# LSH attention, MLP and experts on one core: the sums' transposes and the marks' projections placed behind the products with v, two casts per pair of heads placed behind exponentials

## Chip, cores and metric

The kernel runs on one core of a Trainium2 chip. What counts is the device time of one execution in microseconds; the runs of a kernel are compared by their median. The engines are TensorE (PE; its weight loads are listed apart as PEld), VectorE (DVE), ScalarE (ACT), GpSimd (POOL), and SyncE (SP), which issues most transfers.

## What is computed

Three stages: attention with a mask from hashed buckets, a SiLU MLP, and a layer of eight experts of which each chosen token uses one. The change lies in the first stage, of which this is the reference:

```python
B, H, S, D = q.shape                      # 2, 8, 768, 64
scale = 1.0 / np.sqrt(D)
q_bits = (np.einsum('bhsd,dk->bhsk', q, proj) > 0).astype(np.int64)   # 6 bits
k_bits = (np.einsum('bhsd,dk->bhsk', k, proj) > 0).astype(np.int64)
q_bucket = np.sum(q_bits * powers, axis=-1)
k_bucket = np.sum(k_bits * powers, axis=-1)
mask = q_bucket[:, :, :, None] == k_bucket[:, :, None, :]
scores = np.where(mask, scale * np.matmul(q, k.transpose(0, 1, 3, 2)), -1000000000.0)
scores = scores - np.max(scores, axis=-1, keepdims=True)
attn = np.exp(scores)
attn = attn / (np.sum(attn, axis=-1, keepdims=True) + 1e-09)
return np.matmul(attn, v).astype(np.float32)
```

Behind it come `g = silu(x @ w_in)`, `g @ w_out`, and for the tokens with `x @ w_skip > 0` the expert with the largest gate. All results are float32.

## The kernel before

The sixteen heads are eight pairs i of two heads. Each pair has two halves of its queries; such a half is a unit u (16 in all), and a unit is six steps s: three query tiles of 128 for each of two heads. So there are 96 steps (NS), twelve to a pair; m is the step's place in its pair, and j = s % 3.

A step computes the scores of 128 queries with 768 keys (`em_S`, L407: four matmuls into one of two S buffers in PSUM), their maximum (`em_max`, L412, DVE), the exponential with its sum (`em_exp`, L420, ACT), later the transpose of the probabilities (`em_T`, L431) in groups of three 128x128 pieces, three pieces to one tile "T" in PSUM, and the copy of each T tile into PT in SBUF (`em_C`, L441), some on ACT, some on DVE. In the steps with j = 0 and j = 2 PE turns three T tiles; in those with j = 1 it multiplies a half of a unit's PT with v instead (`em_PV`, L449: 12 instructions, into 64 columns of the array for each head).

Everything runs in the order in which the code is written, engine by engine; nothing is rescheduled. S(s) needs the exponential of step s - 2, since there are two S buffers. The T tiles come from a ring of three PSUM buffers (`tag="T", bufs=3`), which the two kinds of tile below share:

- **rT**: the six reciprocals of a unit's sums (`em_rc`, L453 and L454, in place) are transposed on PE (`em_r`, L460), copied by ACT to r (L462), written to DRAM and read back as rb, spread over the rows; `em_x` multiplies with it on POOL. It stands at the end of step s = 11 + 6u, a step with j = 2.
- **pj**: the bits of the next pair. `prep_proj` (L355) makes four projections, each into 32 columns of the array, and `marked` (L359, DVE) turns them into marks mb, from which seven small DMAs fill rows of Q2 and K2 (`prep_rows`, at m = 4). It stands at the end of the step m = 2, also j = 2.

The next pair's operands are made meanwhile: `PRE` lists the steps m in which ACT casts a head's k and q to K1 and Q1 (L334 and L336, "kh" and "qa"), `POST` those in which DMAs copy them on ("k2", "qb") and POOL subtracts for the low parts ("kl", "ql"). In a step these casts stand ahead of the exponential:

```python
            for mm, *op in PRE[i == 0]:
                if nxt and mm == m:
                    prep_op(i + 1, *op)
            if j == 0 and s <= NS:
                em_C(n0 + 1, onA)
            if s < NS:
                mx = em_max(s)
            if j == 0 and s <= NS:
                em_C(n0, onD)
            if s < NS:
                em_exp(s, mx)
```

In the last third of the attention `hook` slips in the conversion of the first MLP weights (L219 on ACT, L220 to L228 on DVE). `busy` is a zeroed tile that keeps PE at work during the first loads.

Of the kernel before, what the change touches and what calls it, by code (L numbers as in the profile page):

```python
# [9 lines left out]
F32 = mybir.dt.float32  # L10
F32R = mybir.dt.float32r
BF16 = mybir.dt.bfloat16
# [7 lines left out]
P = 128  # L20
# [6 lines left out]
def kernel(  # L27
# [16 lines left out]
    nc = tc.nc  # L44
# [6 lines left out]
    HQ = S // 2  # L51
    QT = HQ // P
# [33 lines left out]
    ident = cp.tile([P, P], F32, name="ident")  # L86
# [190 lines left out]
    def attention(hook):  # L277

        mainp, main_st = opened("a_main")
        evp, ev_st = opened("a_even")  # L280
        topp, top_st = opened("a_top")
        psTV, psTV_st = opened("a_psTV", space=PSUM, side="right")
        psS, psS_st = opened("a_psS", space=PSUM)

        raws, ops, vts, mks = {}, {}, {}, {}
# [64 lines left out]
        def prep_proj(i):  # L350

            ps = psTV.tile([P, HQ], F32, tag="T", name="pj", bufs=3)
            for j in range(4):
                t = raws[i][1 - j // 2]
                nc.tensor.matmul(ps[32 * j:32 * j + 32], prj[j // 2], t[:, (j % 2) * HQ:(j % 2 + 1) * HQ], start=True, stop=True)  # L355
            marked(mks[i], ps, slice(0, P))

        def marked(dst, ps, r):
            nc.vector.tensor_scalar(dst, ps[r], c_m[r, 0:1], c_m[r, 1:2], op0=ALU.is_gt, op1=ALU.mult)  # L359
# [28 lines left out]
        units = [(i, qh) for i in range(B * NP) for qh in range(2)]  # L388
# [4 lines left out]
        NS = len(steps)  # L393
        st_P, st_T, st_sum, st_pv, st_none = {}, {}, {}, {}, {}
# [20 lines left out]
        def em_exp(s, mx):  # L415
            u, qt, hd = steps[s]
            if qt == 0 and hd == 0:
                st_sum[u] = mainp.tile([P, 2 * QT], F32, name="sums", bufs=4)
            pt = mainp.tile([P, S], F32, name="P", bufs=3)
            nc.scalar.activation(pt.rearrange("p (a b) -> p a b", a=2), Ss[s % 2][:, :, 0:HQ], AF.Exp, bias=mx,  # L420
                                 accum_out=st_sum[u][:, hd * QT + qt:hd * QT + qt + 1])
            st_P[s] = pt
# [13 lines left out]
        def em_C(n, copy):  # L436
            if not 0 <= n < 2 * NS:
                return
            s, half = divmod(n, 2)
            u, qt, hd = steps[s]  # L440
            copy(PTs[u % 2][:, hd, half * (KT // 2):(half + 1) * (KT // 2), qt * P:(qt + 1) * P], st_T.pop(n))  # L441

        def em_PV(u, ks):
            i, qh = units[u]
            if 0 in ks:
                st_pv[u] = psTV.tile([P, HQ + 1], F32, tag="V", name="pv", bufs=1)
            for k in ks:
                for hd in range(2):
                    nc.tensor.matmul(st_pv[u][hd * D:(hd + 1) * D], vts[i][:, k, hd], PTs[u % 2][:, hd, k],  # L449
                                     start=(k == 0), stop=(k == KT - 1))  # L450

        def em_rc(u):
            nc.vector.tensor_scalar(st_sum[u], st_sum[u], 1e-9, None, op0=ALU.add)  # L453
            nc.vector.reciprocal(st_sum[u], st_sum[u])  # L454

        def em_r(u):

            sums = st_sum.pop(u)
            ps = psTV.tile([P, HQ], F32, tag="T", name="rT", bufs=3)
            nc.tensor.transpose(ps[0:2 * QT, 0:P], sums, ident)  # L460
            r = mainp.tile([2 * QT, P], F32, name="r", bufs=2)
            nc.scalar.copy(r, ps[0:2 * QT, 0:P])  # L462
            nc.sync.dma_start(r_d[u], r)
            rb = mainp.tile([P, HQ], F32, name="rb", bufs=2)
            for hd in range(2):
                nc.sync.dma_start(rb[hd * D:(hd + 1) * D], r_d[u:u + 1, hd * QT:(hd + 1) * QT].rearrange("o t p -> o (t p)").to_broadcast([D, HQ]))
            return rb

        def em_out(u):

            x = mainp.tile([P, HQ], F32, name="x", bufs=2)
            nc.scalar.activation(x, st_pv.pop(u)[:, 0:HQ], AF.Identity, bias=st_none.pop(u))
            return x
# [16 lines left out]
                eng.tensor_tensor(lo[:, c], x[:, c], hi[:, c].bitcast(F32), op=ALU.subtract)  # L490


        busy = mainp.tile([P, P], BF16, name="busy", bufs=1)
        nc.vector.memset(busy, 0.0)
        bs = psTV.tile([P, P], F32, tag="V", name="bs", bufs=1)

        def em_busy(n):
# [38 lines left out]
        prep_load(1)  # L536
        nc.sync.dma_start(ct[:, 66:NC + P], consts[:, 66:NC + P])
        prep_op(0, 1, "scale", nc.scalar)
        prep_proj(0)
        prep_op(0, 1, "kh", nc.scalar)  # L540
        nc.scalar.copy(Q1[r, 0, c1], qs[r, c1])
        nc.gpsimd.tensor_copy(Q1[o, 0, c1], qs[r, c1])
# [14 lines left out]
        for t in PTs:  # L557
            nc.gpsimd.memset(t[:, :, :, HQ:HQ + 1], 1e-9 / S)

        PRE = [[(c[j], j // 2, w, nc.scalar) for j, w in enumerate(("kh", "qa", "kh", "qa"))]  # L560
               for c in ((0, 3, 6, 9), (3, 5, 7, 9))]

        POST = [[(c[j], j // 4, w, None if w in ("k2", "qb") else nc.gpsimd)
                 for j, w in enumerate(("k2", "kl", "qb", "ql") * 2)]
                for c in ((0, 1, 3, 4, 6, 6, 9, 9), (3, 4, 5, 6, 7, 8, 9, 10))]
        rbs, xs = {}, {}
        onA, onD = nc.scalar.copy, nc.vector.tensor_copy
        for s in range(NS + PU + 4):
            i, m = divmod(s, 2 * PU)
            nxt = i + 1 < B * NP  # L570
            p, j = divmod(s, 3)
            n0 = 6 * p - 5 + (0, 3, 3)[j]
            if nxt and m == 0:
                prep_alloc(i + 1)
            if s < NS:
                if s > 1:
                    em_S(s)
            if j == 0 and s <= NS:
                for n in range(3):
                    em_T(n0 + n)  # L580
            u, g = divmod(s - 10, 6)
            if j == 1 and s < NS and u >= 0:
                em_PV(u, (0, 1, 2) if g == 0 else (3, 4, 5))
            if s == NS:
                em_PV(len(units) - 2, (3, 4, 5))
            if s == NS + 3:
                em_PV(len(units) - 1, range(KT))
            if j == 2 and s < NS or s == NS + 1:
                for n in range(3):
                    em_T(n0 + n)  # L590
                em_C(n0, onA)
                em_C(n0 + 1, onA)
            u, g = divmod(s - 15, 6)
            if g == 0 and 0 <= u < len(units) - 2:
                xs[u] = em_out(u)
            if s == NS + 4:
                xs[len(units) - 1] = em_out(len(units) - 1)
            for mm, *op in PRE[i == 0]:
                if nxt and mm == m:
                    prep_op(i + 1, *op)  # L600
            if j == 0 and s <= NS:
                em_C(n0 + 1, onA)
# [3 lines that stand above are left out]
                em_C(n0, onD)  # L606
            if s < NS:
                em_exp(s, mx)
            if j == 1 and s < NS:
                em_C(n0 - 1, onD)  # L610
            if s == NS:
                em_C(n0 + 2, onD)
            if j == 2 and s < NS:
                em_C(n0 + 2, onD)
            if s == 1:
                prep_op(1, 0, "scale", nc.scalar)
            u, g = divmod(s - 8, 6)
            if g == 0 and 0 <= u < len(units):
                em_rc(u)
            u, g = divmod(s - 14, 6)  # L620
            if g == 0 and 0 <= u < len(units) - 2:
                em_none(u)
            if s == NS + 3:
                em_none(len(units) - 1)
            u, g = divmod(s - 11, 6)
            if s < NS and g == 0 and u >= 0:
                rbs[u] = em_r(u)
            u, g = divmod(s - 17, 6)
            if g == 0 and 0 <= u < len(units) - 1:
                em_x(u, xs.pop(u), rbs.pop(u), nc.gpsimd)  # L630
            if nxt:
                if m == (2 if i else 5):
                    prep_proj(i + 1)
                for mm, *op in POST[i == 0]:
                    if mm == m:
                        prep_op(i + 1, *op)
                if m == (4 if i else 8):
                    prep_rows(i + 1)
                if m == 0 and i + 2 < B * NP:
                    prep_load(i + 2)  # L640
                if m == (9 if i else 11) and i + 2 < B * NP:
                    prep_op(i + 2, 0, "scale", nc.gpsimd)
                if m == 11 and i + 2 < B * NP:
                    load_v(i + 2)
                if m == 11 and i + 2 == B * NP:
                    top_st.close()
            if s == NS - 2 * PU:
                ev_st.close()
            if s == NS:
                em_none(len(units) - 2)  # L650
                xs[len(units) - 2] = em_out(len(units) - 2)
            hook(s - NS)
            if s == NS + PU - 1:
                rbs[len(units) - 1] = em_r(len(units) - 1)
            if s == NS - 1:
                psS_st.close()
        em_x(len(units) - 1, xs.pop(len(units) - 1), rbs.pop(len(units) - 1), nc.gpsimd)
# [277 lines left out]
    with tc.manual_schedule():  # L935
# [130 lines left out]
        ps = ps_tile("pr", [P, 512], "O3")  # L1066
# [352 lines left out]
```

## Time and profile before

| | before |
|---|---|
| median of 3 runs | 607.8 us (607.42 to 609.62) |
| profiled execution | 607.77 us, its span 606.0 us |
| PE busy | 595.2 us (98%) |
| PEld busy | 466.3 us (77%) |
| DVE, ACT, POOL busy | 458.4, 392.1, 188.2 us |
| granted TensorE clock, mean | 0.997 of full speed |

The span is what the trace covers of the profiled execution. PE's busy time counts each matmul with a modelled end, and those overlap; how closely PE's work follows on itself is read from the starts, in the time line. A row of the time line names start, duration, engine, line, operation and tiles, how many were merged (x9), and in brackets the engine's idle time before it and what ended that.

### The profile page before, as it was taken

Reading aid. Unit: us, or ns where it says so; the run is one execution under the profiler, and the core shown is the slowest. Engines: PE = TensorE matmul, PEld = TensorE weight load, DVE = VectorE, ACT = ScalarE, POOL = GpSimd, SP = SyncE. Lnnn points to the kernel's source line nnn. Section 1 sums busy time; section 2 is a strip of 40 time slices with the busy share of each in tenths; the row PEclk is TensorE's granted clock in tenths of the full one; section 3 lists DMA queues with packets and bytes.
Section 4 is the critical chain, followed back from the end, with each engine's and each line's share of the span. In section 5 each row is a group of like instructions: output and inputs, shape, how many; then the busy total and the mean of one; then the engine's idle time right before and its main releaser. Section 6 shows DMA issues by size and latency. Waiting matters only on the chain. (4 is left out here: it accounts for less than half of the span.)

```text
span 606.0 us, 9594 instructions
## 1 busy us (share of the span) xinstructions
PE 595.2 (98%) x3311; PEld 466.3 (77%) x3311; DVE 458.4 (76%) x830; ACT 392.1 (65%) x664; POOL 188.2 (31%) x269
## 2 busy tenths in 40 slices
PE   8999999999999999999999999999999999999996
PEld 6677677676777767888888888888888887888885
DVE  6767767776777777998847985548876649999993
ACT  6878777877877775666544336344445565788872
POOL 7655664657564233300000000300000406344401
PEclk9999999999999999999999999999999999999998
DMA  6541725335131315566423000014231247999960
GB/s 168 147 133 45 202 73 154 104 110 138 48 82 43 129 53 180 189 180 210 158 99 138 1 0 2 1 60 150 104 106 69 53 140 259 321 405 407 405 259 28
DMA packets 31366, 84.13 MB, mean 139 GB/s; under 512 B 6294, under 2 KB 9942, under 8 KB 31186
## 3 DMA queue, kind: packets, MB, share of 16 engines
q1 hardware_dynamic: 29138, 79.44, 39.8%
q0 software_dynamic: 1952, 3.92, 1.9%
q8 instruction: 27, 0.44, 0.3%
q14 instruction: 25, 0.20, 0.1%
q10 hardware_dynamic: 224, 0.13, 0.1%
HBM read 67.92 MB, written 8.50 MB: 126 GB/s over the span
## 5 line engine op out<-in xcount | busy, mean ns | idle before, releaser
L412 DVE TENSOR_REDUCE mx<-S 128x1 f32<-128x770 f32 x96 | 91.8, 957 | 54.6 <-PE S L407 49.3
L260 DVE TENSOR_TENSOR wlo<-wraw,whi 128x1024 fp32r<-128x1024 f32 x100 | 119.7, 1224 | 5.5 <-ACT whi L257 5.0
L257 ACT CAST whi<-wraw 128x1024 fp32r<-128x1024 f32 x100 | 101.6, 1053 | 11.4 <-DVE wraw L228 10.2
L690 ACT ACTIVATE g<-ph 128x512 f32<-128x512 f32 x48 | 28.7, 598 | 106.9 <-PE ph L684 103.0
L420 ACT ACTIVATE P<-S,mx 128x768 f32<-128x768 f32 x96 | 86.8, 905 | 12.3 <-DVE mx L412 11.3
L407 PE MATMUL S<-K,Q 88*128 88x384 f32 (+1 forms) x384 | 91.6, 360 | 2.5 <-ACT P L420 2.0
L407 PEld LDWEIGHTS S<-K,Q 88*128 88x128 f32 (+1 forms) x384 | 62.4, 189 | 27.0 <-issue 18.8
L431 PE MATMUL T<-ident,P 128*128 128x128 f32 x576 | 74.4, 273 | 0.4 <-ACT r L462 0.2
L692 DVE TENSOR_TENSOR gl<-g,gh 128x512 fp32r<-128x512 f32 x48 | 33.2, 691 | 51.9 <-ACT gh L691 51.9
L431 PEld LDWEIGHTS T<-ident,P 128*128 128x128 f32 x576 | 66.8, 141 | 4.1 <-ACT r L462 0.8
L449 PE MATMUL pv<-PT,v 128*64 128x385 f32 x384 | 69.0, 495 | 0.0
L441 ACT COPY PT<-T 128x384 f32<-128x384 f32 x96 | 42.8, 482 | 32.7 <-PE T L431 32.0
L839 POOL DMA_INDIRECT id_d<-tk,slot x12 | 15.7, 1312 | 141.3 <-DVE pre L849 137.9
L348 POOL TENSOR_TENSOR Q<-raw,Q 64x192 fp32r<-64x192 f32 x64 | 36.5, 597 | 54.2 <-ACT Q L336 50.2
L441 DVE COPY PT<-T 128x384 f32<-128x384 f32 x96 | 52.9, 552 | 0.4 <-PE T L431 0.3
L684 PE MATMUL ph<-xhi,whi 128*128 128x512 f32 x192 | 52.2, 393 | 0.0
L684 PE MATMUL ph<-xlo,whi 128*128 128x512 f32 x192 | 51.4, 389 | 0.0
L684 PE MATMUL ph<-xhi,wlo 128*128 128x512 f32 x192 | 51.3, 389 | 0.0
L449 PEld LDWEIGHTS pv<-PT,v 128*64 128x64 f32 x384 | 24.9, 136 | 31.1 <-issue 30.1
L740 DVE CUSTOM_DVE_ANT_0 junk<-x,gwb 128x512 bf16<-128x512 f32 x72 | 45.3, 687 | 0.0
L684 PEld LDWEIGHTS ph<-xlo,whi 128*128 128x128 f32 x192 | 36.0, 188 | 7.6
L684 PEld LDWEIGHTS ph<-xhi,wlo 128*128 128x128 f32 x192 | 36.0, 188 | 7.5
(208 smaller groups left out, 1053.5 us busy)
## 6 DMA issues: line engine op xcount, KB each, us to landing
wraw<-in_w_dram SPq DMA_DIRECT2D x64, 512.0 KB
w<-in_mw_dram SPq DMA_DIRECT2D x32, 512.0 KB
v<-in_vt_dram SPq DMA_DIRECT2D x8, 384.0 KB
rb<-r_d SPq DMA_DIRECT2D x32, 96.0 KB
x_d<-x SPq DMA_DIRECT2D x12, 256.0 KB
out_dram<-x SPq DMA_DIRECT2D x12, 256.0 KB
K<-K SPq DMA_DIRECT2D x15, 192.0 KB
Q<-Q SPq DMA_DIRECT2D x15, 192.0 KB
```

The costliest lines, as they stand in the source:

```text
L257: nc.scalar.copy(hi[:, sl], t[:, sl])
L260: eng.tensor_tensor(lo[:, sl], t[:, sl], hi[:, sl].bitcast(F32), op=ALU.subtract)
L348: eng.tensor_tensor(Q2[0:D, hd, c], raws[i][1][r, c], Q1[r, hd, c].bitcast(F32), op=ALU.subtract)
L407: nc.tensor.matmul(ps[:, c, 0:HQ], q_[0:n, hd, q0:q0 + P], k_[0:n, hd, c * HQ:(c + 1) * HQ], start=first, stop=not first)
L412: nc.vector.tensor_reduce(mx, Ss[s % 2][:, :, 0:HQ + 1], axis=AX.XY, op=ALU.max, negate=True)
L420: nc.scalar.activation(pt.rearrange("p (a b) -> p a b", a=2), Ss[s % 2][:, :, 0:HQ], AF.Exp, bias=mx, accum_out=st_sum[u][:, hd * QT + qt: ...
L431: nc.tensor.transpose(ps[:, j], st_P[s][:, k * P:(k + 1) * P], ident)
L441: copy(PTs[u % 2][:, hd, half * (KT // 2):(half + 1) * (KT // 2), qt * P:(qt + 1) * P], st_T.pop(n))
L449: nc.tensor.matmul(st_pv[u][hd * D:(hd + 1) * D], vts[i][:, k, hd], PTs[u % 2][:, hd, k], start=(k == 0), stop=(k == KT - 1))
L684: nc.tensor.matmul(p_[:, 0:c1 - c0], w[:, k * P:(k + 1) * P], x[:, k, t0 * P + c0:t0 * P + c1], start=(q == 0), stop=(q == len(ops3) - 1))
L692: nc.vector.tensor_tensor(gl[:, c0:c1], g[:, c0:c1], gh[:, c0:c1].bitcast(F32), op=ALU.subtract)
L740: nc.vector.tensor_tensor_reduce(junk, xts[t], pools["gwb_t"][:, c], op0=ALU.mult, op1=ALU.add, scale=1.0, scalar=0.0, accum_out=L[:, t, c ...
```

## The change

The reciprocals go into a tile `rec` of 128 columns, zero beyond the six, and the whole tile is transposed right behind the first group of products with v of a unit (s = 10 + 6u, j = 1); ACT's copy to r and its DMAs follow the exponential of that same step. The projections of pairs 2 and up are placed right behind the second group of products (m = 1), and their marks behind that step's exponential and copy; pair 1's stay where they were. Of the casts of pairs 2 and up, those of m = 3 and 9 are placed in m = 4 and 7, and there behind the exponential; their followers in `POST` move along. `busy` becomes a view of `rec`.

```diff
@@ prep_proj
-            marked(mks[i], ps, slice(0, P))
+            return ps
...
         def em_rc(u):
             nc.vector.tensor_scalar(st_sum[u], st_sum[u], 1e-9, None, op0=ALU.add)
-            nc.vector.reciprocal(st_sum[u], st_sum[u])
-
-        def em_r(u):
-
-            sums = st_sum.pop(u)
+            nc.vector.reciprocal(rec[:, 0:2 * QT], st_sum.pop(u))
+
+        def em_rT():
             ps = psTV.tile([P, HQ], F32, tag="T", name="rT", bufs=3)
-            nc.tensor.transpose(ps[0:2 * QT, 0:P], sums, ident)
+            nc.tensor.transpose(ps[:, 0:P], rec, ident)
+            return ps
+
+        def em_r(u, ps):
+
             r = mainp.tile([2 * QT, P], F32, name="r", bufs=2)
             nc.scalar.copy(r, ps[0:2 * QT, 0:P])
             nc.sync.dma_start(r_d[u], r)
...
-        busy = mainp.tile([P, P], BF16, name="busy", bufs=1)
-        nc.vector.memset(busy, 0.0)
+        rec = mainp.tile([P, P], F32, name="rec", bufs=1)
+        nc.vector.memset(rec, 0.0)
+        busy = rec.bitcast(BF16)[:, 0:P]
...
         PRE = [[(c[j], j // 2, w, nc.scalar) for j, w in enumerate(("kh", "qa", "kh", "qa"))]
-               for c in ((0, 3, 6, 9), (3, 5, 7, 9))]
+               for c in ((0, 4, 6, 7), (3, 5, 7, 9))]
...
-                for c in ((0, 1, 3, 4, 6, 6, 9, 9), (3, 4, 5, 6, 7, 8, 9, 10))]
+                for c in ((0, 1, 4, 4, 6, 6, 7, 8), (3, 4, 5, 6, 7, 8, 9, 10))]
...
             if j == 1 and s < NS and u >= 0:
                 em_PV(u, (0, 1, 2) if g == 0 else (3, 4, 5))
+                if g == 0:
+                    rT = em_rT()
+                if nxt and m == 1 and i:
+                    pj = prep_proj(i + 1)
...
-            for mm, *op in PRE[i == 0]:
-                if nxt and mm == m:
+            casts = [op for mm, *op in PRE[i == 0] if nxt and mm == m]
+            if j != 1 or i == 0:
+                for op in casts:
                     prep_op(i + 1, *op)
...
             if s < NS:
                 em_exp(s, mx)
+            u, g = divmod(s - 10, 6)
+            if s < NS and g == 0 and u >= 0:
+                rbs[u] = em_r(u, rT)
+            if j == 1 and i:
+                for op in casts:
+                    prep_op(i + 1, *op)
             if j == 1 and s < NS:
                 em_C(n0 - 1, onD)
+            if nxt and m == 1 and i:
+                marked(mks[i + 1], pj, slice(0, P))
...
-            u, g = divmod(s - 11, 6)
-            if s < NS and g == 0 and u >= 0:
-                rbs[u] = em_r(u)
...
-                if m == (2 if i else 5):
-                    prep_proj(i + 1)
+                if m == 5 and not i:
+                    marked(mks[1], prep_proj(1), slice(0, P))
...
             if s == NS + PU - 1:
-                rbs[len(units) - 1] = em_r(len(units) - 1)
+                rbs[len(units) - 1] = em_r(len(units) - 1, em_rT())
```

On PE, the first unit with both moves, before (steps 10 to 14; S_109 and S_110 are the two S buffers, "x9" is three T tiles):

```order
L449 MATMUL pv<-PT_111,v 64x385 x6
L407 MATMUL S_110<-K_132,Q_131 128x384 x2
L407 MATMUL S_110<-K_107,Q_133 128x384 x2
L431 MATMUL T<-ident,P 128x128 x9
L460 MATMUL rT<-ident,sums 6x128
L407 MATMUL S_109<-K_252,Q_251 128x384 x2
...
L449 MATMUL pv<-PT_111,v 64x385 x6
L407 MATMUL S_109<-K_252,Q_251 128x384 x2
L407 MATMUL S_109<-K_108,Q_253 128x384 x2
L431 MATMUL T<-ident,P 128x128 x9
L355 MATMUL pj<-raw,ct 32x384 x4
```

The same stretch of PE after the change:

```order
L449 MATMUL pv<-PT_111,v 64x385 x6
L458 MATMUL rT<-ident,rec 128x128
L407 MATMUL S_110<-K_132,Q_131 128x384 x2
L407 MATMUL S_110<-K_107,Q_133 128x384 x2
L431 MATMUL T<-ident,P 128x128 x9
...
L449 MATMUL pv<-PT_111,v 64x385 x6
L355 MATMUL pj<-raw,ct 32x384 x4
L407 MATMUL S_109<-K_252,Q_251 128x384 x2
L407 MATMUL S_109<-K_108,Q_253 128x384 x2
L431 MATMUL T<-ident,P 128x128 x9
```

Both extra tiles move from behind nine transposes to behind six products, ahead of the next S; rT grows from 6 rows of output to 128.

On ACT, the steps m = 3 to 7 of the second pair, before (K_502 and Q_501 are K1 and Q1 of the next pair):

```order
L472 ACTIVATE x<-pv,none 128x384
L336 CAST Q_501<-raw 64x768
L441 COPY PT_111<-T 128x3x128
L420 ACTIVATE P,sums<-S_110,mx 128x768
L420 ACTIVATE P,sums<-S_109,mx 128x768
L441 COPY PT_111<-T 128x3x128 x2
L420 ACTIVATE P,sums<-S_110,mx 128x768
L462 COPY r<-rT 6x128
L334 CAST K_502<-raw 64x768
```

The same steps of ACT after the change, up to the second cast that moves:

```order
L474 ACTIVATE x<-pv,none 128x384
L441 COPY PT_111<-T 128x3x128
L420 ACTIVATE P,sums<-S_110,mx 128x768
L420 ACTIVATE P,sums<-S_109,mx 128x768
L464 COPY r<-rT 6x128
L336 CAST Q_501<-raw 64x768
L441 COPY PT_111<-T 128x3x128 x2
L420 ACTIVATE P,sums<-S_110,mx 128x768
L334 CAST K_502<-raw 64x768
L441 COPY PT_111<-T 128x3x128
...
L420 ACTIVATE P,sums<-S_110,mx 128x768
L336 CAST Q_501<-raw 64x768
```

The casts to Q1 stand no longer between x and a copy that an exponential waits behind, but between an exponential and the copies of the next step's T tiles, the first of them behind the copy to r.

## Rows read from the trace of the kernel before

**Rows 1.** Busy time by stage: us, then each engine's busy time, 24 to 223 us.

```profile
24.00:223.00 199.00, 198.12 (x1304) 141.07 (x1304) 144.20 (x248) 154.18 (x329) 110.69 (x179) 1.00 0.36 99
```

**Rows 2.** Time line of PEld, a T group and the next S.

```profile
105.40 1.08 PEld L431 LDWEIGHTS T<-ident,P 128*128 128x128 f32 x9
106.45 0.65 PEld L407 LDWEIGHTS S<-K,Q 128*128 128x128 f32 x4
```

**Rows 3.** Waits of PEld for other engines, 215 to 592 us: total, times, longest.

```profile
PEld L803 <- DVE oh L791: 0.7, 1, 0.7
...
PEld ey L1209 <- DVE wlo L260: 0.3, 1, 0.3
```

**Rows 4.** Time line of PEld around rT, two units.

```profile
97.16 1.08 PEld L431 LDWEIGHTS T<-ident,P 128*128 128x128 f32 x9
...
98.40 0.19 PEld L407 LDWEIGHTS S<-K,Q 128*128 128x128 f32 x1
...
137.63 1.08 PEld L431 LDWEIGHTS T<-ident,P 128*128 128x128 f32 x9
...
138.94 0.65 PEld L407 LDWEIGHTS S<-K,Q 128*128 128x128 f32 x4
```

**Rows 5.** Waits of PEld, 24 to 215 us: total, times, longest.

```profile
PEld S L407 <- ACT P L420: 4.4, 6, 0.8
PEld rT L460 <- ACT PT L441: 1.6, 10, 0.2
PEld pj L355 <- ACT PT L441: 1.0, 6, 0.2
```

**Rows 6.** Time line of PEld around pj.

```profile
89.84 1.08 PEld L431 LDWEIGHTS T<-ident,P 128*128 128x128 f32 x9
91.08 0.16 PEld L355 LDWEIGHTS pj<-raw,ct 128*32 128x32 f32 x8 [0.17 <-ACT PT L441]
91.87 0.64 PEld L407 LDWEIGHTS S<-K,Q 128*128 128x128 f32 x4 [0.62 <-issue]
```

**Rows 7.** Time line of PEld, the end of a pv group and S.

```profile
95.47 0.14 PEld L449 LDWEIGHTS pv<-PT,v 128*64 128x64 f32 x2 [0.18 <-issue]
95.79 0.14 PEld L449 LDWEIGHTS pv<-PT,v 128*64 128x64 f32 x2 [0.18 <-issue]
96.53 0.64 PEld L407 LDWEIGHTS S<-K,Q 128*128 128x128 f32 x4 [0.60 <-issue]
```

**Rows 8.** Time line of PEld, two waits for ACT.

```profile
109.63 0.65 PEld L407 LDWEIGHTS S<-K,Q 128*128 128x128 f32 x4 [0.79 <-ACT P L420]
...
113.25 0.31 PEld L431 LDWEIGHTS T<-ident,P 128*128 128x128 f32 x3 [0.30 <-ACT r L462]
```

**Rows 9.** Time line of PEld at the attention's end.

```profile
217.46 1.08 PEld L431 LDWEIGHTS T<-ident,P 128*128 128x128 f32 x9
...
220.78 0.20 PEld L449 LDWEIGHTS pv<-PT,v 128*64 128x64 f32 x4 [0.17 <-issue]
```

**Rows 10.** DVE: a maximum, the marks (ns min/median/max), a copy near the end.

```profile
90.28 0.96 DVE L412 TENSOR_REDUCE mx<-S 128x1 f32<-128x770 f32 x1 [1.56 <-PE S L407]
...
L359 DVE TENSOR_SCALAR mb<-pj,ct x8: 676/677/678, 8.6 to 173.6; 128x384 fp32r<-128x384 f32 x8
...
218.95 0.54 DVE L441 COPY PT<-T 128x384 f32<-128x384 f32 x1
```

**Rows 11.** Time line of ACT: copies, r, an exponential, a cast.

```profile
97.86 0.86 ACT L441 COPY PT<-T 128x384 f32<-128x384 f32 x2 [1.25 <-PE T L431]
...
99.49 0.24 ACT L462 COPY r<-rT 6x128 f32<-6x128 f32 x1
...
105.16 0.92 ACT L420 ACTIVATE P<-S,mx 128x768 f32<-128x768 f32 x1
...
107.23 0.83 ACT L336 CAST Q<-raw 64x768 fp32r<-64x768 f32 x1
```

**Rows 12.** Time line of DVE at the start: the memset of the warming tile.

```profile
0.84 0.11 DVE L494 MEMSET busy<- 128x64 uint32 x1 [0.84 <-PEq L1407]
```

More of the change, by code (lines that the diff above doesn't have):

```diff
@@ L538, in attention @@
         prep_op(0, 1, "scale", nc.scalar)
-        prep_proj(0)
+        marked(mks[0], prep_proj(0), slice(0, P))
         prep_op(0, 1, "kh", nc.scalar)
```

## The prediction

> **What bounds the kernel now.** I read the stages first, then who waits for whom, then the time line of the weight loads, which shows when TensorE really turns to its next group. From 24 to 223 us, the attention after its start, PE is busy 198.12 of 199 us, ACT 154.18 and DVE 144.20 [rows 1]. A busy PE is not yet a PE at its peak, so the reader should look at the starts of groups instead. A step without extras is S (4 loads), then T (9 transposes), and the next S starts 1.05 us after T did (106.45 - 105.40) [rows 2]: the tempo of the engine itself. Whatever makes such a distance longer is time that the whole program pays, since nothing else ends late: behind the attention the waits of the weight loads for other engines are 0.7 and 0.3 us [rows 3].
>
> Three things make it longer. Behind the sums' transposes (rT) the distance is 1.24 us (98.40 - 97.16), and 1.31 where a new pair begins (138.94 - 137.63), so 0.19 and 0.26 more [rows 4]; the loads wait there for ACT's copy PT, 1.6 us in ten cases [rows 5]. The reason is the ring of three T buffers: T, T, T have just taken all three, so a fourth tile must wait until ACT has emptied the first. The marks' projections (pj) stand in the same position: 91.87 - 89.84 = 2.03, so 0.98 more than a plain step, of which pj itself to the next S is 0.79 (91.87 - 91.08) and 0.19 lies ahead of it, again with ACT PT as the releaser [rows 5, 6]. Thirdly, S behind a pv group waits for the exponential two steps back: 0.79 us idle instead of the usual 0.60 [rows 7, 8], so 0.19. Such waits make 4.4 us in six cases [rows 5]; six times the usual 0.60 is 3.6, and the 0.8 left is four times 0.19. They lie in the pairs in which the conversion of MLP weights puts one more ACT instruction ahead of that stretch.
>
> **The change, part by part.** *Sums' transposes.* Fifteen are moved in the loop; I count fourteen here and the last below. Seven lose 0.19 and seven 0.26 (every other unit ends a pair). What they pay in the new place: one more full transpose behind pv, 1.05 / 9 = 0.12 us each [rows 2]; the seam from pv to something full-width exists already (S today, rT then). Its buffer there is the first tile of the T group before, which DVE copied long before pv ends, so no wait. Sum: 7 x (0.19 - 0.12) + 7 x (0.26 - 0.12) = 1.5 us gained. Bounds: 3.2 if the transpose vanishes under the seam (7 x 0.19 + 7 x 0.26), 0.1 if leaving it costs a second seam of 0.10 each (below).
>
> *End of the attention.* The two T groups with rT between them take 220.78 - 217.46 = 3.32 us up to pv [rows 9]. The row at 113.25 shows the kind of wait inside: T stands until ACT has copied r out of rT's buffer [rows 8]. With rT gone from there, the last three transposes need only DVE's copy of the first group's third tile, which ends at 218.95 + 0.54 = 219.49 [rows 10]; three transposes (0.35) on top and a little for the semaphore put pv at 219.9, so 0.87 less, minus 0.12 for the moved one: 0.75. Bounds: 0, if the waits only change their name, and 3.32 - 2 x 1.05 - 0.12 = 1.1.
>
> *Projections.* Six are moved (the first pair's stays). Each gives back 0.98. In the new place it costs 0.79 up to the S behind it, if the seam from pv to pj is as long as that from pv to S. That seam can be priced: pairs of pv start 0.32 apart (95.79 - 95.47), loads run one pair ahead, so the last pair would be through at 95.79 + 2 x 0.32 = 96.43, and S starts at 96.53: 0.10 [rows 7]. No row has pv followed by another column-tiled group. With the seam the gain is 0.98 - 0.79 = 0.19, without it 0.29: 1.1 or 1.7 us in all. I take 1.1, since the nearest row, pv to S, has the seam. The Trainium skill, TensorEngine Tiling (Array Packing), Key Properties, says that a change of tiling mode drains the engine; pv has 64 columns and pj 32, so by it the seam is there and the part is worth 1.1; if the seam came only between tiled and full it would be 1.7.
> DVE's marks (0.68 us) wait for pj behind the copy of that step and stand ahead of the next maximum; DVE idles 1.56 us there today and pj makes the hole longer [rows 10]. The third T tile of the next step needs the buffer which the marks free; by the starts [rows 6] it would want it some 1.3 us behind the S after pj, and the marks end about 0.8 behind it. So nothing is paid.
>
> *Casts, and r's copy, on ACT.* Two casts a pair (0.83 each) go from in front of an exponential behind one, into the hole in which ACT waits for PE's transposes: 1.25 us idle at 97.86 [rows 11]. In the one step that gets both r's copy (0.24) and a cast the sum is 1.07, so it fits, barely once PE's result for r is waited for. The cast at 107.23 sits in front of the exponential that S at 109.63 waits for; with it gone, the four waits of 0.19 (0.76) go. The single T wait for r at 113.25, 0.30 idle [rows 8], goes with the buffer's earlier release: 0.28 net of the ordinary spacing. Together 1.0 us; bounds 0 and 1.1. What is late next in that stretch is nothing: a step's exponential ended at 105.16 + 0.92 = 106.08 and its S started at 106.45 [rows 2, 11], 0.37 of slack.
>
> *At nothing.* r's three DMAs move on SP ahead of the qb copy and the seven DMAs of the marks; those are due at the next pair, some eight steps of two us later, so a round trip of a few us is covered; without that cover the next pair's S would wait for them. POOL's subtractions and DVE's converts follow their inputs and have whole steps. Ahead of the first matmul a memset of 0.11 us gets twice as wide [rows 12]: at most 0.11 lost, once. The last unit's transpose costs 0.12 more at worst.
>
> Sum: 1.5 + 0.75 + 1.1 + 1.0 = 4.35, say 4.4 us. The profiled execution took 607.77 us (span 606.0), and the median of the runs is 607.8, the same: 607.8 - 4.4 = **603.4 us**.
>
> **The rivals.** *The seams eat it.* If a full transpose between pv and S costs a second seam of 0.10, and pj too, the first part falls to 0.1 and the third to 0.5 (six times 0.10 less), and the time is 607.8 - (0.1 + 0.75 + 0.5 + 1.0) = 605.4. For it: no row shows a full-width matmul alone between pv and S. Against it: at the attention's end T follows pv today and pays one seam only.
> *Taken back downstream.* If the MLP waited for converted weights rather than for PE, an earlier attention would buy idle time: 607.8, no change. Against it stand the waits of [rows 3]: after the attention PE hardly waits for anything.
> *ACT gets late: slower.* The two j = 1 casts and r's copy stand in front of the PT copies and the exponential of the next step. If PE reached its transposes before ACT was through, the whole 1.07 would push that exponential, 0.37 of it free, 0.70 paid, and 0.83 - 0.37 = 0.46 at the other cast: 6 x 1.16 = 7.0 us, so 603.4 + 7.0 = 610.4. It decides from the point at which ACT's hole in those steps is shorter than 1.07 less 0.37 = 0.70 us. Today's 1.25 speaks against it [rows 11], and the hole gets longer, not shorter, behind rT.
>
> **How the numbers follow.** The forecast, 602.3 to 604.5 (0.9 to 1.1 either way: about half of the way to the ends of the first three parts, which need not fall together), has 0.70. The seams rival, 604.5 to 606, has 0.14; the no-change rival 0.08; the slower one 0.04; 0.04 remains for over 5.5 us gained, with pj's seam absent and rT hidden. From 601.9 to 605.9 leaves out no more than 2 in 10. A measurement of this kernel tells about 0.5%, 3.0 us, from no change, so faster means below 604.8: 0.70 + 0.04 + a quarter of the seams rival, 0.77. Slower by over 0.5% is 0.04, and the rest, 0.19, is same.
>
> **What would show it.** In the profile after: the distance from T to the next S is 1.05 everywhere in the attention, with no rT or pj row in between; from the start of pv to the S behind rT 2.09 + 0.12; from pv's start to the S behind pj about 2.09 + 0.79; no PEld row that waits for ACT PT or ACT r; S behind pv with 0.60 idle in all pairs, and T to pv at the attention's end 2.3 to 2.6 us. The MLP's stretches should keep their length and merely start earlier. I am wrong if rT or pj brings a gap of its own beyond these, if the exponentials of the steps behind the moved casts start later relative to their S, or if a new wait of PE appears behind 223 us.

## The result and the profile after

The changed kernel took 602.78 us (median of 4 runs, 602.73 to 603.04); runs of the kernel before on the same chip had a median of 608.59 (607.42 to 609.62). The ratio is 0.9906 with a 95% interval of 0.9884 to 0.9928, so it is faster by 0.9%. The prediction was 603.4 us. The profiled span went from 606.0 to 601.0 us. Runs of one kernel lie at two levels some 2 us apart, and two of the four before lie at the upper one while all four after, and both profiled executions, lie at the lower, so the change itself is worth the 5.0 us between the spans, 0.8%.

The attention's stretch first, as in [rows 1]: busy time by stage, of the kernel after.

```profile
24.00:218.50 194.50, 194.49 (x1309) 141.21 (x1307) 148.61 (x248) 155.75 (x329) 113.84 (x178) 1.00 0.36 103
```

It shows the same engines as full as before; PE's work has merely fewer holes. Where they were is in the time line of PEld of the kernel after, around a unit with rT (to be read against [rows 4] and [rows 7]):

```profile
94.71 0.14 PEld L458 LDWEIGHTS rT<-ident,rec 128*128 128x128 f32 x1 [0.60 <-issue]
94.72 0.72 PEld L407 LDWEIGHTS S<-K,Q 128*128 128x128 f32 x4
95.42 1.08 PEld L431 LDWEIGHTS T<-ident,P 128*128 128x128 f32 x9
96.47 0.65 PEld L407 LDWEIGHTS S<-K,Q 128*128 128x128 f32 x4
```

rT starts with the 0.60 idle that S had behind pv, S is loaded at once behind it, and from T to the next S it is 1.05 us where it was 1.24. The four loads of S take 0.72 instead of 0.64 to 0.65: so the transpose costs 0.06 to 0.07 us here. The projections, against [rows 6]:

```profile
87.57 0.16 PEld L355 LDWEIGHTS pj<-raw,ct 128*32 128x32 f32 x8 [0.60 <-issue]
88.35 0.65 PEld L407 LDWEIGHTS S<-K,Q 128*128 128x128 f32 x4 [0.62 <-ACT P L420]
88.99 1.08 PEld L431 LDWEIGHTS T<-ident,P 128*128 128x128 f32 x9
90.03 0.65 PEld L407 LDWEIGHTS S<-K,Q 128*128 128x128 f32 x4
```

pj also has the gap of 0.60, and 0.78 us to the next S; from T to S it is 1.04. The waits of PEld from 24 to 215 us, against [rows 5]:

```profile
PEld pv L449 <- issue: 26.6, 139, 0.3
PEld rT L458 <- issue: 7.8, 13, 0.6
PEld S L407 <- issue: 6.0, 10, 0.6
PEld pj L355 <- issue: 3.6, 6, 0.6
PEld S L407 <- ACT P L420: 2.5, 4, 0.6
PEld pv L449 <- ACT x L474: 1.5, 5, 0.3
```

No rT or pj waits for ACT PT any more; what stands there now is the gap of 0.60 that S had. The four S that name ACT's exponential stand behind pj with 0.62 us idle each, which is what S had there before without that name (91.87 in [rows 6]), so they lose nothing to it. The end of the attention, against [rows 9]:

```profile
213.26 1.07 PEld L431 LDWEIGHTS T<-ident,P 128*128 128x128 f32 x9
214.49 1.10 PEld L431 LDWEIGHTS T<-ident,P 128*128 128x128 f32 x9 [0.15 <-ACT PT L441]
215.75 0.20 PEld L449 LDWEIGHTS pv<-PT,v 128*64 128x64 f32 x4 [0.17 <-issue]
...
218.45 0.77 PEld L697 LDWEIGHTS ph<-xhi,whi 128*128 128x128 f32 x4
```

From T to pv it is 215.75 - 213.26 = 2.49 us instead of 3.32. The second group still waits 0.15 us for ACT's copy of a T tile (214.49), since its first tile stands behind three others in the same ring of three. The MLP's first product (ph) began at 223.48 before, in this row of that kernel's time line,

```profile
223.48 0.76 PEld L684 LDWEIGHTS ph<-xhi,whi 128*128 128x128 f32 x4
```

so it comes 5.03 us earlier, and the program ends 5.0 earlier: in this execution nothing is given back in the MLP and the experts.

### The profile page after: what moved, and what is told of

The parts are those of the page before. It is cut to its first block, busy times and chain, and to the rows that moved or that the text cites. A ratio compares the mean times of both kernels' runs of the same rounds, so it can differ in the third digit from the quotient of the medians.

```text
span 601.0 us, 9588 instructions
## 1 busy us (share of the span) xinstructions
PE 591.7 (98%) x3311; PEld 466.4 (78%) x3311; DVE 463.2 (77%) x830; ACT 394.0 (66%) x664; POOL 190.0 (32%) x269
## 4 chain that ended last, share of the span: by engine, by line
PE 92%; DVE 2%; DMA 2%; issue 1%; ACT 1%; POOL 0%; POOLq 0%; SPq 0%; DVEq 0%; ACTq 0%
PE ph L697 22%; PE o L740 14%; PE S L407 11%; PE pv L449 11%; PE T L431 10%; PE o L731 7%; PE eh L1200 5%; PE ey L1222 5%; PE tr L1177 1%; PE pj L355 1%; DVE wlo L260 1%; DMA wraw<-in_w_dram 1%; PE rT L458 1%; ACT P L420 1%; PE bs L503 1%
## 5 line engine op out<-in xcount | busy, mean ns | idle before, releaser
L348 POOL TENSOR_TENSOR Q<-raw,Q 64x192 fp32r<-64x192 f32 x64 | 39.1, 639 | 56.9 <-ACT Q L336 53.0
```

## The experiments

For each kernel the table has the start of the S of step 11 and of the MLP's first ph, from PEld's time line, and the distance: the attention without its start. I compare by this distance, since in the profiles of three kernels (casts_back, casts_only, two_casts) the first 12 us take some 2 us longer than in the others, with nothing of the experiments in them (last section).

| kernel | S of step 11 | first ph | distance | span | median of runs |
|---|---|---|---|---|---|
| before | 28.66 | 223.48 | 194.82 | 606.0 | 607.8 (607.62 to 609.32 beside the others) |
| changed | 28.34 | 218.45 | 190.11 | 601.0 | 602.78 |
| e1_rT_back | 28.34 | 221.88 | 193.54 | 604.5 | 606.44 |
| e2_rT_narrow | 28.25 | 217.64 | 189.39 | 600.7 | 602.14 |
| e3_pj_back | 28.51 | 219.77 | 191.26 | 602.4 | 604.06 |
| e4_casts_back | 30.19 | 220.57 | 190.38 | 603.2 | 603.45 |
| e5_rT_first | 28.33 | 220.65 | 192.32 | 603.2 | 605.01 |
| e6_casts_only | 30.36 | 224.55 | 194.18 | 607.1 | 608.69 |
| e7_kh_too | 28.63 | 218.73 | 190.10 | 601.5 | 603.53 |
| e8_two_casts | 30.88 | 225.25 | 194.38 | 607.8 | 609.04 |
| e9_changed_again | 28.45 | 218.56 | 190.12 | 601.1 | 603.13 |
| e10_narrow_again | 28.11 | 217.49 | 189.38 | 601.5 | 602.82 |

The change as a whole is worth 194.82 - 190.11 = 4.71 us of this distance; e9 repeats it to 0.01.

**Place or shape of the sums' transpose.** My theory was the ring: behind three T tiles the fourth tile has no buffer until ACT has copied the first. The rival was the shape: six columns among full-width transposes.

```diff
 # e1_rT_back: changed kernel
-                if g == 0:
-                    rT = em_rT()
...
+            u, g = divmod(s - 11, 6)
+            if s < NS and g == 0 and u >= 0:
+                rbs[u] = em_r(u, em_rT())
```

> The changed kernel with only rT put back to the end of the step with j = 2, behind its nine transposes, still 128 columns wide; all else as changed. Ring theory (behind three T tiles the ring of three buffers is full, so rT waits for ACT's first PT copy): the place alone matters, so the 2.2 us that the in-loop transposes gave and the 0.75 at the attention's end are lost, span 601.0 + 2.9 = 603.9 us, and PEld rT waits for ACT PT in all cases. Shape theory (the six-column transpose among full-width ones cost the time, the wait for ACT only coincides): the width is kept, so the span stays within 0.5 of 601.0.

The distance is 3.43 us longer than the changed kernel's (the ratio to before is 0.997, 0.9953 to 0.9987). That is 0.5 more than expected: from S to S, the seven steps with m = 6 take 1.74 to 1.75 us instead of 1.69, and the one step in which T waits for r again is 0.15 longer. PEld of e1, one unit:

```profile
96.25 1.08 PEld L431 LDWEIGHTS T<-ident,P 128*128 128x128 f32 x9
97.48 0.14 PEld L458 LDWEIGHTS rT<-ident,rec 128*128 128x128 f32 x1 [0.15 <-ACT PT L441]
97.48 0.71 PEld L407 LDWEIGHTS S<-K,Q 128*128 128x128 f32 x4
```

The full width waits for ACT PT in the old place as the narrow one did, T to S is 1.23 again. The shape theory falls on this, and the next two runs take it apart from both sides.

```diff
 # e2_rT_narrow: changed kernel
-            nc.tensor.transpose(ps[:, 0:P], rec, ident)
+            nc.tensor.transpose(ps[0:2 * QT, 0:P], rec[:, 0:2 * QT], ident)
```

> The changed kernel with rT in its new place behind pv, but only the six columns transposed, as before the change. Ring theory: span 601.0, at most 0.5 off, distance from pv's start to the S behind rT as in the changed kernel. Shape theory: 14 transposes get a second seam of 0.10 to 0.20 us back, span 602.4 to 603.8.

Shorter than the changed kernel by 0.72 us, which neither theory had said; the span of 600.7 lies in the ring theory's range. The rows of e2, and below them those of the changed kernel at the same unit:

```profile
41.77 0.08 PEld L458 LDWEIGHTS rT<-ident,rec 128*6 128x6 f32 x1 [0.60 <-issue]
41.77 0.65 PEld L407 LDWEIGHTS S<-K,Q 128*128 128x128 f32 x4
42.41 1.09 PEld L431 LDWEIGHTS T<-ident,P 128*128 128x128 f32 x9
```

```profile
41.90 0.14 PEld L458 LDWEIGHTS rT<-ident,rec 128*128 128x128 f32 x1 [0.60 <-issue]
41.90 0.72 PEld L407 LDWEIGHTS S<-K,Q 128*128 128x128 f32 x4
42.60 1.08 PEld L431 LDWEIGHTS T<-ident,P 128*128 128x128 f32 x9
```

The narrow load takes 0.08 us and S is through in 0.64 (42.41 - 41.77); the full one takes 0.14, and S needs 0.70 (42.60 - 41.90). So the width costs about 0.05 a unit, and a narrow transpose behind pv costs nothing that shows: it starts where S would have, 0.60 behind pv, and S is loaded at the same instant. The other side is the old kernel with the place changed, within the same step. ACT's copy to r moves along; it reads rT, so it cannot be what rT itself waited for:

```diff
 # e5_rT_first: kernel before
+            u, g = divmod(s - 11, 6)
+            if s < NS and g == 0 and u >= 0:
+                rbs[u] = em_r(u, em_rT(u))      # transpose, and ACT's copy
             if j == 2 and s < NS or s == NS + 1:
                 for n in range(3):
                     em_T(n0 + n)
```

> The kernel before, with rT (six columns, as it was) ahead of the three T tiles of its step instead of behind them, and ACT's copy to r ahead of its PT copies. It still stands among full-width transposes and no cast is moved. Ring theory: rT finds a free buffer, so 2 to 3 us are gained from the place alone, span 606.0 - 2.5 = 603.5, and no PEld rT waits for ACT PT. Shape theory: nothing gained, 606.0.

The distance is 2.50 us shorter than before's (ratio 0.9958, 0.9944 to 0.9973). PEld of e5:

```profile
96.30 0.08 PEld L459 LDWEIGHTS rT<-ident,sums 128*6 128x6 f32 x1
96.47 1.01 PEld L431 LDWEIGHTS T<-ident,P 128*128 128x128 f32 x9
97.45 0.65 PEld L407 LDWEIGHTS S<-K,Q 128*128 128x128 f32 x4
```

Six columns, between S and T, no wait, and 1.15 from rT to the next S. The ring theory is shown: with the shape as it was and no cast moved, turning nine and one into one and nine takes the wait away. That the number of buffers sets the place of the wait is argued from the kernel and from the releaser in the rows; no run changed that number.

**The projections.**

```diff
 # e3_pj_back: changed kernel
-                if nxt and m == 1 and i:
-                    pj = prep_proj(i + 1)
...
+                if m == (2 if i else 5):
+                    marked(mks[i + 1], prep_proj(i + 1), slice(0, P))
```

> The changed kernel with only the projections and marks put back to the end of m = 2. Ring theory: six times 0.20 us lost, span 602.2, and PEld pj waits for ACT PT again. If the projections' place is worth nothing and the gain came from ACT's relief: 601.0.

Longer by 1.15 us, as expected; PEld pj waits for ACT PT again (1.0 us, six times):

```profile
88.76 1.08 PEld L431 LDWEIGHTS T<-ident,P 128*128 128x128 f32 x9
90.00 0.16 PEld L355 LDWEIGHTS pj<-raw,ct 128*32 128x32 f32 x8 [0.17 <-ACT PT L441]
90.78 0.64 PEld L407 LDWEIGHTS S<-K,Q 128*128 128x128 f32 x4 [0.62 <-issue]
```

**The casts.** Once taken out of the changed kernel, once put alone into the kernel before:

```diff
 # e4_casts_back: changed kernel             # e6_casts_only: kernel before, the other way round
-               for c in ((0, 4, 6, 7), (3, 5, 7, 9))]
+               for c in ((0, 3, 6, 9), (3, 5, 7, 9))]
-                for c in ((0, 1, 4, 4, 6, 6, 7, 8), (3, 4, 5, 6, 7, 8, 9, 10))]
+                for c in ((0, 1, 3, 4, 6, 6, 9, 9), (3, 4, 5, 6, 7, 8, 9, 10))]
```

> The changed kernel with only the casts (and their followers) put back to m = 0, 3, 6, 9 in front of the exponentials. Theory: only the S behind pv at m = 10 of four pairs waits again, 0.13 to 0.19 each, and a T or two; 0.5 to 1.0 us lost, span 601.5 to 602.0. Rival (ACT's relief carries the whole change): 2 us lost or more, 603 and up.

> The kernel before with only the casts and their followers moved to m = 4 and 7 behind the exponentials; rT and pj stay. Theory: the four waits of 0.19 behind pv at m = 10 go and the single wait of T for r, 0.5 to 1.1 us gained, span 605.0 to 605.5. Rival (ACT's relief carries the change): 3 us or more, 603 or less.

e4 loses 0.27 us, half of the least that I had expected; e6 gains 0.64 in the attention, though its runs (ratio 1.0008, 0.9994 to 1.0022) don't show it. By the spans, e4's 603.2 would fit the rival and e6's 607.1 neither of the two; but in these executions the S of step 11 starts 1.85 and 1.70 us later than in the kernel each was made from, ahead of every cast that was moved. The rows of e4 at the place of [rows 8] tell why the sum of the parts is not the whole:

```profile
108.69 0.14 PEld L449 LDWEIGHTS pv<-PT,v 128*64 128x64 f32 x2 [0.18 <-issue]
109.43 0.14 PEld L458 LDWEIGHTS rT<-ident,rec 128*128 128x128 f32 x1 [0.60 <-DVE PT L441]
109.62 0.65 PEld L407 LDWEIGHTS S<-K,Q 128*128 128x128 f32 x4
```

S starts 0.19 behind rT there, 0.00 to 0.01 elsewhere: the exponential is late as before, but rT now runs in that time. Moving rT had already taken part of the casts' gain. In e6 the four waits of S behind pv are gone and the wait of T for r remains (0.29 us), as it belongs to rT. The four pairs are those in which ACT runs one conversion of MLP weights (L219), at 79.0, 106.0, 133.4 and 160.5 us of the kernel before; so the hook begins well before the last third of the attention.

**One cast more, and one too many.** e7 puts the first head's kh from m = 0 to m = 1 (PRE (1, 4, 6, 7)), e8 the second head's from m = 6 to m = 4 (PRE (0, 4, 4, 7)).

> The changed kernel with one more cast moved: the first head's kh goes from m = 0, in front of the exponential, to m = 1 behind it, where pj makes ACT's hole longest; its copy k2 follows at m = 1. Theory: the waits left at m = 0 and 10 of the pairs with MLP conversion (0.03 to 0.13 each) go, 0.2 to 0.4 us gained, span 600.7. Rival: the hole is full, or the copies come late, and an S of the next pair waits: 601.5 or more.

Distance 190.10 against 190.11: nothing. The span of 601.5 would fit the rival, but what it has over 601.0 lies ahead of step 11 (0.29 us) and behind the first ph (0.2). The waits left at m = 10 do not come from that cast: there pv itself waits until ACT has read the last unit's products out of pv's buffer into x (L474), in the changed kernel

```profile
105.48 0.20 PEld L449 LDWEIGHTS pv<-PT,v 128*64 128x64 f32 x4 [0.33 <-ACT x L474]
```

with 0.28 to 0.33 us idle in the four pairs with a conversion, where 0.24 to 0.25 is the rule; in e7 it is 0.28 to 0.34.

> The changed kernel with the second head's kh moved from m = 6 to m = 4 as well, so that r's copy and two casts stand in one hole of ACT. In the changed kernel that hole is just full: the cast ends at about 96.07 and the PT copies start at 96.12. If the tipping point of the slower rival is right (0.37 us of slack, the rest paid by an S), the second cast of 0.83 costs 0.46 in each of six pairs, the S of m = 7 waits for the exponential, and the span is 601.0 + 2.8 = 603.8 us. If ACT has more room than that: 601.0 to 601.5.

Slower, and by more than the 2.8 us that I had worked out: the distance is 4.27 us longer, 0.71 in each of six pairs. ACT of the changed kernel in that step, then PEld of e8:

```profile
95.24 0.83 ACT L336 CAST Q<-raw 64x768 fp32r<-64x768 f32 x1
96.12 0.86 ACT L441 COPY PT<-T 128x384 f32<-128x384 f32 x2
96.87 0.92 ACT L420 ACTIVATE P<-S,mx 128x768 f32<-128x768 f32 x1
```

```profile
101.43 0.97 PEld L431 LDWEIGHTS T<-ident,P 128*128 128x128 f32 x9 [0.36 <-ACT PT L441]
102.83 0.65 PEld L407 LDWEIGHTS S<-K,Q 128*128 128x128 f32 x4 [0.43 <-ACT P L420]
```

Two waits, not one: T stands 0.36 us for a ring buffer that ACT's late copy frees, and then S for the late exponential. Only some 0.1 of the second cast's 0.83 is free (0.83 - 0.71), not 0.37.

**The better version.** Narrow and full side by side again:

> The changed kernel once more, beside the next one on the same chip: 602.8 us.

> The changed kernel with the six-column transpose in the new place once more: 14 times 0.055 us less than the one beside it, so 602.0 us. If the first difference was chance: 602.8.

The narrow one's distance is 0.74 us shorter (0.72 the first time), the medians are 602.82 for it and 603.13. The timed runs alone could not tell the two apart (ratios to before 0.9908, 0.9888 to 0.9929, and 0.9922, 0.9901 to 0.9944); the trace can, for the attention, and twice the same way. At the end of the program the profiles show the gain in part or not at all: from the first ph to the end the narrow version took 600.7 - 217.64 = 383.06 us in e2 and 601.5 - 217.49 = 384.01 in e10, the changed kernel 601.0 - 218.45 = 382.55. What is lost lies in the experts, at a transpose that waits for the DMA of its gathered tokens, here in e10:

```profile
524.41 0.63 PE L1177 MATMUL tr<-ident,xg 128*128 128x128 f32 x4 [1.04 <-DMA xg<-x_d,eid]
```

Whether the earlier attention brings this wait or the executions merely differ there is not shown. The fastest run of the narrow version took 602.04 us both times, that of the full one 602.73 and 602.61. I would keep the six-column transpose: shorter in the attention, and no slower in the runs.

## Why the prediction was right

*What bounds it* held: every hole that the change took out of PE's stream in the attention came out of the span, 5.03 us by the first ph and 5.0 at the end. The rival "taken back downstream" is gone with that, for this change. Of the 5.03, 0.32 lies ahead of step 11 (28.66 against 28.34) and was no part of the forecast; the repeat e9 had 28.45, so it varies.

*Sums' transposes*: predicted 1.5. The starts of S behind the fourteen units move by 0.12 to 0.20 each, 2.2 in all. The step that was mis-sized is "one more full transpose behind pv, 1.05 / 9 = 0.12 us each": it costs about 0.06 (S through in 0.70 instead of 0.64), and e2 shows the narrow one at nothing. rT starts where S did, behind the same gap, and S is loaded at once; what hides the other half of the 0.12 is not shown. The seams rival fell the same way, as rT to S has no gap (94.71 to 94.72).

*End of the attention*: predicted 0.75; from S of step 95 to ph it was 223.48 - 216.83 = 6.65 before and 218.45 - 212.56 = 5.89 after, 0.76. The way there was not quite the one forecast: the second group was to need only DVE's copy, and no weight load was to wait for ACT PT, but one still does, 0.15 us (214.49).

*Projections*: predicted 1.1; e3 measured 1.15. The seam from pv to pj, which no row of before showed, is there: 0.60 idle, as from pv to S, against 0.18 between pairs of pv. The Trainium skill (TensorEngine Tiling (Array Packing), Key Properties) states that changing the tiling mode drains the engine, and this row agrees with it for pv to pj.

*Casts*: "Together 1.0 us" was too much. Alone they bring 0.64 (e6), on top of the rest 0.27 (e4). I had added the four waits to the rest as if rT did not run in the same time, and the wait of T for r to the casts' account although it goes with rT. 2.2 + 0.76 + 1.15 leave 0.6 of the 4.71 for them; the removals cannot settle how that is to be shared.

*The sum*: 0.7 us too little for the transposes and 0.4 too much for the casts partly cancel, so 4.35 comes within 0.36 of the measured 4.71; that much is luck.

*At nothing*: no new wait of any size stands behind the moved transfers; DVE's marks and the longer SP chain cost nothing that the trace shows. One of the named signs of being wrong did appear, though. Behind a cast at m = 7 the exponential starts later relative to its S, 103.40 - 101.15 = 2.25 us in the kernel after,

```profile
101.15 0.64 PEld L407 LDWEIGHTS S<-K,Q 128*128 128x128 f32 x4 [0.60 <-issue]
103.40 0.90 ACT L420 ACTIVATE P<-S,mx 128x768 f32<-128x768 f32 x1
```

against 105.16 - 103.09 = 2.07 before ([rows 11] for the exponential):

```profile
103.09 0.64 PEld L407 LDWEIGHTS S<-K,Q 128*128 128x128 f32 x4 [0.60 <-issue]
```

ACT's conversion and x follow that exponential, so x is late too, and pv's wait for it at m = 10 is the price: 0.03 to 0.08 us in four pairs.

*The slower rival* had the right mechanism and a wrong tipping point. The change puts 1.07 us into ACT's hole and just fits: the cast ends at 96.07 (95.24 + 0.83), the copies start at 96.12. I had looked at the slack of the exponential alone; the T ring is a second path from the same copies back to PE.

## What to carry to other kernels

When an engine is full, look at the starts of its groups rather than at its busy time, and ask of each long distance which buffer the next group waits for: here a fourth tile behind three in a ring of three cost about 0.2 us each time, and the same tile ahead of the three did not wait. Behind a group that is followed by a gap anyway, as pv is here, a small matmul can cost nothing and a wide one little (0.00 and 0.06 us, in these runs). Work that is moved into another engine's idle hole should be measured against that hole by all paths that lead out of it, buffers as well as data, before a second piece is added.

## What the hardware showed beyond that

A load that follows another shape need not wait: behind the six-column transpose S is loaded at once (41.77 and 41.77), while behind the 32-column projections it has 0.62 idle (91.87 in [rows 6]).

Executions can differ by 2 us in their first 12 us. PE in e4_casts_back, and in the changed kernel:

```profile
4.92 0.84 PE L523 MATMUL S<-raw,ct 64*32 64x384 f32 x1
...
7.79 0.97 PE L503 MATMUL bs<-rec 128*128 128x128 bf16 x7
...
9.97 0.80 PE L407 MATMUL S<-K,Q 88*128 88x384 f32 x3
```

```profile
4.92 0.64 PE L523 MATMUL S<-raw,ct 64*32 64x384 f32 x1
...
6.60 0.56 PE L503 MATMUL bs<-rec 128*128 128x128 bf16 x7
...
8.17 1.13 PE L407 MATMUL S<-K,Q 88*128 88x384 f32 x5
```

The same matmuls, with nothing of the experiment in them, take longer in the one execution than in the other, the seven on rec 0.97 us instead of 0.56, and by the last row shown it is 1.8 us behind, while the granted clock reads 1.00, the level of 2.4 GHz, from 4.5 to 10.5 us in both. Why is open.
